# Late weight loads held back until tile 15 is transposed, engine orders judged under noise, and readout work moved from VectorE and ScalarE to GpSimd and VectorE

## The chip, the cores and the metric

The kernel runs on one core of one Trainium2 chip. Times are device microseconds (us). A time quoted for a kernel is the median of its runs; the span, which the profile shows, is about 1.7 us shorter and reaches from the first to the last instruction of one execution.

Engines in the profile lines: PE = TensorE matmuls, PEld = TensorE weight loads, DVE = VectorE, ACT = ScalarE, POOL = GpSimd, SP = the engine that issues most DMAs here.

## The reference

Two kinds of layer alternate, A, B, A, B, with the same weights in both rounds. `x` is [1, 2048, 512] in bf16; there are 32 heads of 16 elements; F is 1376.

```python
def _A_ref(x, wqkv, w_phi, wo):            # linear attention; H = 32, Dh = 16
    qkv = ...(x @ wqkv)...                 # q, k, v per head
    pq = einsum("bhsd,hdf->bhsf", q, w_phi); pk = einsum("bhsd,hdf->bhsf", k, w_phi)
    phi_q = concatenate([softmax(pq), softmax(-pq)], -1)
    phi_k = concatenate([softmax(pk), softmax(-pk)], -1)
    kv = einsum("bhsf,bhsd->bhfd", phi_k, v)
    z  = einsum("bhsf->bhf", phi_k)        # sum over all rows s
    num = einsum("bhqf,bhfd->bhqd", phi_q, kv)
    den = einsum("bhqf,bhf->bhq", phi_q, z)[..., None] + 1e-6
    return (num / den)...reshape(B, S, D) @ wo

def _B_ref(x, W_gate, W_up, W_down):
    gate = x @ W_gate; gate = gate * (gate > 0)
    return (gate * (x @ W_up)) @ W_down

x = A_x
x = x + _A_ref(_layernorm(x), ...);  x = x + _B_ref(_layernorm(x), ...)
x = x + _A_ref(_layernorm(x), ...);  x = x + _B_ref(_layernorm(x), ...)
```

The sum over all rows in `kv` divides each A layer in two. First comes a **key phase**, which ends with the last accumulation of `kv`; then a **readout**, which gives `num / den` tile by tile and feeds the **feed-forward** of layer B.

## The kernel before

The program works on 16 tiles of 128 rows. It is recorded as a list of operations, each with an engine, a modelled duration, and the things that it reads and writes. A list scheduler then makes one fixed order per engine: it tries 4 weights x 12 passes and keeps the order with the shortest modelled makespan.

```python
best = None
for weight in self.ORDER_WEIGHTS:
    prio = [weight * o.idx - rank[o.idx] - o.boost for o in ops]
    for _ in range(self.PASSES):
        start, finish, order = self._forward(prio)
        span = max(finish)                          # the judge
        if best is None or span < best[0]:
            best = (span, start, finish, order)
        prio = [t - o.boost for t, o in zip(self._backward(start, finish), ops)]
```

In the key phase of the first layer, VectorE makes layer-norm statistics and the softmax sums `Zk`, ScalarE the exponentials, and GpSimd multiplies by the reciprocal sums. The SP queue carries the DMA transposes of the normalised tiles (`yT`) and, between them, the weights that only later phases need.

```python
# knorm (per tile): sums and reciprocal on VectorE, then the product on GpSimd
op("dve", tensor_reduce(Zk, expk)); op("dve", reciprocal(rZk, Zk))
parts = [("pool", 0, 2)] if t < NT - 2 else [("pool", 0, 1), ("dve", 1, 2)]   # last two tiles split

def kv(t, n):                                       # emit(), layer 0
    ...
    for tt in range(t, t + n):
        self.kv_acc(tt, "A0")
        for _ in range(1 if 4 <= tt < 12 else 2):   # 8 wo, 4 Wg, 4 Wu, 6 Wd pieces
            if pieces:
                pieces.pop(0)(self.r("phik", tt, 0))
L(1); kv(0, 1); kv(1, 1); L(2); kv(2, 1); kv(3, 1); self.compose_q(); kv(4, 2)
L(3)                                                # layer norms and transposes, tiles 12 to 15
kv(6, 2); kv(8, 2); kv(10, 2); self.q_proj(0, qr0, "A0"); kv(12, 2); kv(14, 1); kv(15, 1)
```

The readout of one tile copies three groups of `num` out of PSUM on ScalarE, does the division on VectorE, transposes the result by DMA, and multiplies by `wo`.

```python
for gb in range(3):
    ...                                             # 8 matmuls in all
    op("act", activation(numbf[gb], psum, Copy))                         # numcp
op("dve", tensor_tensor(zm, nv, nr, mult))          # 64 columns
op("dve", tensor_tensor(zd, zm[0:32], zm[32:64], add))
op("dve", reciprocal(zr, zd))
op("dve", tensor_tensor(ab, nr, zr, mult))
op("dve", tensor_tensor(tsc, numbf, ab, mult))      # 1024 columns
op("dve", tensor_tensor(osb, tsc[0:512], tsc[512:1024], add))
self.dma_tr(oT <- osb)                              # SP queue
...                                                 # 4 matmuls with wo, residual add on VectorE
```

(The calls above are abridged; the names are the program's.)

The softmax here doesn't subtract the row's maximum and nothing guards it: scores larger than these inputs give would overflow.

## Time and profile before

| | before |
|---|---|
| time, median of 3 runs | 396.07 us (395.46 to 396.57) |
| span of the profiled execution | 394.1 us |
| last key accumulation, layer 0 (start of its last matmul; the modelled end is 0.22 us later) | 54.30 us |
| first gate matmul, layer 1 | 74.85 us |
| last key accumulation, layer 2 | 242.69 us |
| first gate matmul, layer 3 | 261.60 us |

The first line below is the busy time of each engine, from the page of the kernel before. The rows after it are the window view of the same execution: start and end of the stretch and its length, then busy us (and count of instructions) of PE, PEld, DVE, ACT and POOL, granted clock, share of the DMA engines, and GB/s.

```profile
PE 381.1 (97%) x2320; PEld 207.1 (53%) x2320; DVE 274.3 (70%) x634; ACT 215.8 (55%) x421; POOL 110.1 (28%) x160
...
15.00:55.00 40.00, 38.13 (x279) 20.89 (x277) 35.57 (x56) 31.92 (x48) 33.15 (x24) 1.00 0.66 161
55.00:65.00 10.00, 7.79 (x58) 4.13 (x57) 8.14 (x27) 8.79 (x17) 0.00 (x0) 1.00 0.18 43
65.00:76.00 11.00, 11.00 (x70) 5.98 (x68) 9.37 (x28) 10.43 (x16) 2.81 (x6) 1.00 0.30 60
76.00:240.00 164.00, 164.00 (x958) 88.13 (x957) 122.95 (x266) 75.54 (x159) 51.74 (x74) 1.00 0.18 34
240.00:257.00 17.00, 15.89 (x141) 9.71 (x139) 13.42 (x43) 13.73 (x25) 2.60 (x5) 1.00 0.16 32
257.00:270.00 13.00, 13.00 (x102) 9.07 (x100) 11.26 (x33) 11.52 (x25) 2.38 (x6) 1.00 0.34 65
```

TensorE has all of the 164 us in the middle. It has room in the key phase (15 to 55), in the first 10 us of the readout (55 to 65, where ScalarE is the busiest engine with 8.79 of 10 us), and in the same place of layer 2 (240 to 257).

Matmul ends are modelled, so a second measure is used throughout: the **loss**. That is the spacing of successive matmul starts beyond the normal spacing for their shape, summed over a window (the normal is the median in the trace of the kernel before: 216 ns for 128x512, 109 for 128x256, 63 for 128x144, 56 for 128x129 and 107 for the 128x128 ones, most of which come in the first 15 us). It is 12.8 us over the whole execution. The Trainium skill, "Perfetto Trace Analysis", Identifying the Most-Contended Engine, also calls matmul busy share a bad measure of how near a kernel is to its limit. This trace agrees in the small: 55 to 65 shows 2.2 us without a busy matmul, but 3.3 us of loss.

What TensorE waited for in the key phase, 15 to 55 us, from the view of waits (us in total, times, longest):

```profile
PE ps L587 <- DMA yT<-ytile: 1.2, 2, 0.9
PE ps L602 <- POOL expk L573: 0.3, 1, 0.3
```

And the starts of the readout in the timeline, 55 to 66 us (start, length, instruction, and in brackets the idle time before it with what ended it):

```profile
60.17 1.16 PE L645 MATMUL ps<-kvbd,expq 128*128 128x144 bf16 x8 [0.60 <-ACT numbf L649]
...
62.07 0.60 PE L675 MATMUL ps<-wo_p,oT 128*128 128x512 bf16 x2 [0.74 <-DMA oT<-osb]
...
64.22 0.60 PE L629 MATMUL ps<-yT,Wqp 128*128 128x512 bf16 x2 [0.68 <-ACT expq L632]
```

So the key phase waits for transposed tiles (L587 is the key projection), and at its end for GpSimd's product (L573). The readout waits twice for ScalarE (a `numbf` copy, an exponential `expq`) and once for a transposed output tile.

The costs that the argument needs, from the groups by shape (busy us and mean ns of one, then the idle time before):

```profile
L573 POOL TENSOR_TENSOR expk<-expk,rZk 128x1024 bf16<-128x1024 bf16 x28 | 53.6, 1933 | 30.1 <-DVE rZk L570 14.8 <-ACT expk L559 4.9 <-ACT vsb L561 4.3
...
L669 DVE TENSOR_TENSOR osb<-tsc 128x512 bf16<-128x512 bf16 x32 | 13.4, 418 | 0.2
L649 ACT ACTIVATE numbf<-ps 128x288 bf16<-128x288 f32 x32 | 13.4, 418 | 2.1 <-PE ps L645 2.1
```

### The profile page before, as it was taken

How to read it: one execution, taken by the hardware profiler on the slowest of the kernel's cores; microseconds unless marked ns; L12 is line 12 of the kernel's file. 1: busy time of each engine (PE TensorE's matmuls, PEld its weight loads, DVE VectorE, ACT ScalarE, POOL GpSimd, SP SyncE). 2: the span in 40 equal slices, each digit the busy share in tenths (PEclk: the TensorE clock that was granted, in tenths of full speed). 3: DMA queues.
4: the chain of work that ended last, by engine and by line, in shares of the span. 5: the costliest groups of instructions: out<-in, count | busy, mean ns of one | idle time of the engine just before them, and what ended most of it. 6: DMA issues, size and time to landing. Idle time of an engine off the chain costs nothing.

```text
span 394.1 us, 6313 instructions
## 1 busy us (share of the span) xinstructions
PE 381.1 (97%) x2320; PEld 207.1 (53%) x2320; DVE 274.3 (70%) x634; ACT 215.8 (55%) x421; POOL 110.1 (28%) x160
## 2 busy tenths in 40 slices
PE   5998997999999999999999999899999999999996
PEld 3455463676744444444444457467774454444442
DVE  5999778886865888886765777997875576421332
ACT  5897769953744412633354475997573562453440
POOL 5399741211000122383344543121101011100000
PEclk9999999999999999999999999999999999999999
DMA  6845942221211222311100110232323122100001
GB/s 189 217 86 147 240 146 53 55 54 28 55 28 27 42 54 54 68 27 15 27 14 2 27 28 2 41 68 54 68 55 67 27 42 67 29 27 0 28 27 53
DMA packets 61518, 23.00 MB, mean 58 GB/s; under 512 B 53456, under 2 KB 60464, under 8 KB 61488
## 3 DMA queue, kind: packets, MB, share of 16 engines
q1 hardware_dynamic: 60912, 22.08, 24.7%
q10 hardware_dynamic: 576, 0.52, 0.5%
q8 instruction: 18, 0.29, 0.3%
q14 instruction: 12, 0.10, 0.1%
HBM read 7.91 MB, written 2.10 MB: 25 GB/s over the span
## 4 chain that ended last, share of the span: by engine, by line
PE 83%; DVE 7%; issue 3%; DMA 3%; ACT 2%; POOL 2%; SPq 0%; DVEq 0%; POOLq 0%
PE ps L696 39%; PE ps L720 19%; PE ps L556 7%; PE ps L675 7%; PE ps L629 5%; PE ps L645 3%; PE ps L602 2%; DVE stats L516 2%; POOL expk L573 2%; DVE rZk L570 1%; DMA yT<-ytile 1%; DVE Zk L568 1%; DMA x_sb<-in_A_x_dram 1%; ACT numbf L649 1%; DMA oT<-osb 1%
## 5 line engine op out<-in xcount | busy, mean ns | idle before, releaser
L696 PE MATMUL ps<-yT,Wu 128*128 128x512 bf16 (+3 forms) x440 | 128.2, 336 | 0.0
L696 PE MATMUL ps<-yT,Wg 128*128 128x512 bf16 (+3 forms) x440 | 128.0, 336 | 0.0
L698 ACT ACTIVATE gate_sb<-ps 128x512 bf16<-128x512 f32 (+3 forms) x110 | 55.8, 512 | 100.8 <-PE ps L696 86.1
L720 PE MATMUL ps<-Wd,hT 128*128 128x512 bf16 (+1 forms) x352 | 107.7, 379 | 0.0
L573 POOL TENSOR_TENSOR expk<-expk,rZk 128x1024 bf16<-128x1024 bf16 (+1 forms) x32 | 59.6, 1879 | 31.6 <-DVE rZk L570 16.2
L520 POOL TENSOR_SCALAR rv<-mv 128x1 f32<-128x1 f32 (+1 forms) x55 | 13.0, 238 | 190.1 <-DVE mv L517 187.7
L696 PEld LDWEIGHTS ps<-yT,Wu 128*128 128x128 bf16 (+1 forms) x440 | 43.8, 100 | 33.4 <-ACT expk L703 0.8
L696 PEld LDWEIGHTS ps<-yT,Wg 128*128 128x128 bf16 (+1 forms) x440 | 43.5, 100 | 33.4 <-ACT gate_sb L698 0.9
L649 ACT ACTIVATE numbf<-ps 128x432 bf16<-128x432 f32 (+1 forms) x96 | 44.1, 500 | 18.1 <-PE ps L645 16.9
L720 PEld LDWEIGHTS ps<-Wd,hT 128*128 128x128 bf16 (+1 forms) x352 | 34.1, 98 | 36.8 <-DVE x_sb L722 0.9
L705 DVE TENSOR_TENSOR hT<-gate_sb,expk 128x512 bf16<-128x512 bf16 (+3 forms) x73 | 25.9, 355 | 34.2 <-ACT expk L703 33.0
L516 DVE BATCH_NORM_STATS2 stats<-x_sb 128x6 f32<-128x512 bf16 x64 | 42.7, 683 | 4.8 <-DMA x_sb<-in_A_x_dram 4.5
L568 DVE TENSOR_REDUCE Zk<-expk 128x64 f32<-128x1024 bf16 x32 | 37.9, 1202 | 6.3 <-ACT expk L559 3.1
L675 PE MATMUL ps<-wo_p,oT 128*128 128x512 bf16 x128 | 39.9, 379 | 1.6 <-DMA oT<-osb 1.6
L722 DVE TENSOR_TENSOR x_sb<-x_sb,ps 128x512 bf16<-128x512 bf16 x32 | 21.7, 685 | 27.1 <-PE ps L720 27.0
L703 ACT ACTIVATE expk<-ps 128x512 bf16<-128x512 f32 (+3 forms) x73 | 36.1, 497 | 1.1 <-PE ps L696 1.0
L645 PE MATMUL ps<-kvbd,expq 128*128 128x144 bf16 x256 | 35.1, 226 | 0.9 <-ACT numbf L649 0.6
L629 PE MATMUL ps<-yT,Wqp 128*128 128x512 bf16 x128 | 34.7, 379 | 0.9 <-ACT expq L632 0.7
L521 POOL TENSOR_TENSOR rstd<-rv,mhalf 128x1 f32<-128x1 f32 (+1 forms) x55 | 34.0, 620 | 4.1
L632 ACT ACTIVATE expq<-ps 128x1024 bf16<-128x1024 f32 (+1 forms) x40 | 32.4, 858 | 4.2 <-PE ps L629 3.8
L708 DVE TENSOR_TENSOR hT<-gate_sb,ps 128x512 bf16<-128x512 bf16 (+2 forms) x37 | 22.6, 614 | 16.8 <-PE ps L696 14.4
L559 ACT ACTIVATE expk<-ps 128x512 bf16<-128x512 f32 x44 | 23.8, 596 | 19.2 <-PE ps L556 18.9
(57 smaller groups left out, 393.3 us busy)
## 6 DMA issues: line engine op xcount, KB each, us to landing
out_dram<-x_sb SPq DMA_DIRECT2D x16, 128.0 KB, 1.7
x_sb<-in_A_x_dram SPq DMA_DIRECT2D x3, 512.0 KB, 6.1
Wg<-in_B_W_gate_dram SPq DMA_DIRECT2D x4, 344.0 KB, 4.2
Wu<-in_B_W_up_dram SPq DMA_DIRECT2D x4, 344.0 KB, 4.5
Wd<-in_B_W_down_dram SPq DMA_DIRECT2D x5, 256.0 KB, 3.3
yT<-ytile SPq DMA_TRANSPOSE x60, 2.4
hT<-in_A_wqkv_dram ACTq DMA_DIRECT2D x4, 128.0 KB, 3.0
x_sb<-in_A_x_dram SPq DMA_DIRECT2D x4, 128.0 KB, 3.7
```

Source lines behind the costliest of these rows:

```text
L516: op("dve", (lambda t: lambda e: e.bn_stats(k.stats6[:, t, :], k.x_sb[:, t, :]))(t), [r("x", t)], [r("st", t)], 685, f"{tag} stats {t}")
L521: op("pool", lambda e: e.tensor_tensor(k.rstd[:, t0:t1, :], k.rv1[:, t0:t1, :], k.mhalf[:, 0:n], ALU.pow), [r("rv1", t) for t in ts] + [r( ...
L568: op("dve", lambda e: e.tensor_reduce(k.Zk[:, zb, :], k.expk[:, t, :, :].rearrange("p s (h f) -> p (s h) f", f=16), AX.X, ALU.add), [r("ex ...
L573: op(eng, (lambda s0, s1: lambda e: e.tensor_tensor(k.expk[:, t, s0:s1, :].rearrange("p s (h f) -> p (s h) f", f=16), k.expk[:, t, s0:s1, ...
L629: op("pe", (lambda c, ic, bank: lambda e: e.matmul(k.pb[bank][:], k.Wqp[:, ic, c * 128:(c + 1) * 128], k.yT[:, ic, st * 512:(st + 1) * 512 ...
L645: op("pe", (lambda s, c, j, g0, bank: lambda e: e.matmul(k.pb[bank][:, j * GW:(j + 1) * GW], k.expq[:, st, c, s, tt * 128:(tt + 1) * 128], ...
L649: op("act", (lambda g0, n, bank: lambda e: e.activation(k.numbf[:, b, g0:g0 + n, :], k.pb[bank][:, 0:n * GW].rearrange("p (g m) -> p g m", ...
L675: op("pe", (lambda c, bank: lambda e: e.matmul(k.pb[bank][:], k.oT[:, ob, c, :], k.wo_p[:, c, :], start=(c == 0), stop=(c == NC - 1)))(c, ...
L696: op("pe", (lambda bank, W, ic, fc, Mf: lambda e: e.matmul(k.pb[bank][0:Mf, 0:n], W[:, ic, fc * 128:fc * 128 + Mf], k.yT[:, ic, c0:c0 + n] ...
L698: op("act", (lambda Mf, gb, gs: lambda e: e.activation(k.gate_sb[0:Mf, gs, 0:n], k.pb[gb][0:Mf, 0:n], ACT.Relu))(Mf, gb, gs), [self.RP[gb] ...
L703: op("act", (lambda Mf, ub, tu: lambda e: e.activation(k.expk[0:Mf, tu, 0, 0:n], k.pb[ub][0:Mf, 0:n], ACT.Copy))(Mf, ub, tu), [self.RP[ub] ...
L720: op("pe", (lambda fc, Kf, u, c0: lambda e: e.matmul(k.pb[bank][:], k.hT[0:Kf, u, c0:c0 + 128], k.Wd[0:Kf, fc, :], start=(fc == 0), stop=( ...
```

## The change

It has three parts. The *late weights* no longer depend on the tiles' products one by one: all of them wait for the transpose of tile 15. The *order* is judged by a replay under noise (six sets of durations, each within 8%) in place of the modelled makespan. In the *readout*, the third `numbf` copy goes from ScalarE to VectorE for every tile, and four small operations (`zm`, `zd`, `ab`, `osb`) go from VectorE to GpSimd from the third tile on.

```diff
@@ schedule
+        rng = random.Random(1)
+        noise = [[rng.uniform(0.92, 1.08) for _ in ops] for _ in range(self.TRIALS)]   # TRIALS = 6
-                span = max(finish)
+                span = self._replay(order, noise)
@@ num (calls cut)
-            op("act", activation(numbf, ..., Copy), 165 + n * 120, numcp)
+            op("dve" if gb == 2 else "act", evac(numbf, ...), 165 + n * (150 if gb == 2 else 120), numcp)
+        sm = "dve" if t < 2 else "pool"
-        op("dve", zm ...);  op("dve", zd ...);  op("dve", ab ...);  op("dve", osb ...)
+        op(sm, zm ...);     op(sm, zd ...);     op(sm, ab ...);     op(sm, osb ...)
@@ emit
             for tt in range(t, t + n):
                 self.kv_acc(tt, "A0")
-                for _ in range(1 if 4 <= tt < 12 else 2):
-                    if pieces:
-                        pieces.pop(0)(self.r("phik", tt, 0))
@@
         L(3)
+        for i, piece in enumerate(pieces):
+            piece(self.r("yT", 15 if i < 8 else 15))
```

(The body of `_replay` runs the fixed order through the model with scaled durations and returns the mean makespan.)

More of the change, by code (lines that the diff above doesn't have):

```diff
@@ L1 @@
+import random
 from contextlib import ExitStack
@@ L53 @@
     PASSES = 12
+    TRIALS = 6
     DMA_BW = 240.0
@@ L141, in schedule @@
                 prio = [t - o.boost for t, o in zip(self._backward(start, finish), ops)]
-        self.makespan, start, finish, order = best
+        _, start, finish, order = best
+        self.makespan = max(finish)
         for o in ops:
@@ L201, in _forward, with _replay @@
         return start, finish, order
+    def _replay(self, order, noise):
+        ops = self.ops
+        total = 0.0
+        for f in noise:
+            free = {e: 0.0 for e in ENG_NAMES}
+            fin = [0.0] * len(ops)
+            q_free = 0.0
+            for i in order:
+                o = ops[i]
+                t = free[o.eng]
+                for d in o.deps:
+                    t = max(t, fin[d] + (self.SAME_LAT if ops[d].eng == o.eng else self.SYNC_LAT))
+                free[o.eng] = t + o.dur * f[i]
+                if o.is_dma:
+                    q_free = max(t + self.DMA_FIXED * 0.35, q_free) + o.dma_bytes / self.DMA_BW * (3 * f[i] - 2)
+                    fin[i] = q_free + self.DMA_FIXED * 0.65 * (5 * f[i] - 4)
+                else:
+                    fin[i] = free[o.eng]
+            total += max(fin)
+        return total / len(noise)
     def _backward(self, start, finish):
@@ L335, with evac @@
 WINDOW = {"sp": 24, "act": 64, "pe": 400, "dve": 40, "pool": 24}
+def evac(e, out, in_):
+    return e.activation(out, in_, ACT.Copy) if hasattr(e, "activation") else e.tensor_copy(out, in_)
 class Kernel:
@@ L648, in num @@
                    [r("expq", st, c, s), r("kvbd", gb), r("kvones")], [self.RP[bank]], 63, f"{tag} num {t} {g0 + j}")
-            op("act", (lambda g0, n, bank: lambda e: e.activation(
-                k.numbf[:, b, g0:g0 + n, :], k.pb[bank][:, 0:n * GW].rearrange("p (g m) -> p g m", m=GW), ACT.Copy))(g0, n, bank),
-               [self.RP[bank]], [r("numbf", b, gb)], 165 + n * 120, f"{tag} numcp {t} {gb}")
+            op("dve" if gb == 2 else "act", (lambda g0, n, bank: lambda e: evac(
+                e, k.numbf[:, b, g0:g0 + n, :], k.pb[bank][:, 0:n * GW].rearrange("p (g m) -> p g m", m=GW)))(g0, n, bank),
+               [self.RP[bank]], [r("numbf", b, gb)], 165 + n * (150 if gb == 2 else 120), f"{tag} numcp {t} {gb}")
         RN = [r("numbf", b, gb) for gb in range(3)]
@@ L654, in num @@
         nr = nv[:, ::-1, :, 136:144]
-        op("dve", lambda e: e.tensor_tensor(
+        sm = "dve" if t < 2 else "pool"
+        op(sm, lambda e: e.tensor_tensor(
             k.zm[:, b, :].rearrange("p (s c h) -> p s c h", s=2, h=8), nv[:, :, :, 128:136], nr, ALU.mult),
-           RN, [r("zm", b, 0), r("zm", b, 1)], 222, f"{tag} zm {t}")
-        op("dve", lambda e: e.tensor_tensor(k.zd[:, b, :], k.zm[:, b, 0:32], k.zm[:, b, 32:64], ALU.add), [r("zm", b, 0), r("zm", b, 1)], [r("zd", b)], 190, f"{tag} zd {t}")
+           RN, [r("zm", b, 0), r("zm", b, 1)], 222 if sm == "dve" else 310, f"{tag} zm {t}")
+        op(sm, lambda e: e.tensor_tensor(k.zd[:, b, :], k.zm[:, b, 0:32], k.zm[:, b, 32:64], ALU.add), [r("zm", b, 0), r("zm", b, 1)], [r("zd", b)], 190 if sm == "dve" else 270, f"{tag} zd {t}")
         op("dve", lambda e: e.reciprocal(k.zr[:, b, :], k.zd[:, b, :]), [r("zd", b)], [r("zr", b)], 350, f"{tag} zr {t}")
-        op("dve", lambda e: e.tensor_tensor(
+        op(sm, lambda e: e.tensor_tensor(
             k.ab[:, b, :].rearrange("p (s c h) -> p s c h", s=2, h=8), nr,
             k.zr[:, b, :].rearrange("p (c h) -> p c h", h=8).unsqueeze(1).to_broadcast([P, 2, 4, 8]), ALU.mult),
-           RN + [r("zr", b)], [r("ab", b, 0), r("ab", b, 1)], 222, f"{tag} ab {t}")
+           RN + [r("zr", b)], [r("ab", b, 0), r("ab", b, 1)], 222 if sm == "dve" else 310, f"{tag} ab {t}")
         op("dve", lambda e: e.tensor_tensor(
@@ L668, in num @@
            RN + [r("ab", b, 0), r("ab", b, 1)], [r("tsc", b)], 690, f"{tag} tsc {t}")
-        op("dve", lambda e: e.tensor_tensor(k.osb[:, b, :], k.tsc[:, b, 0:512], k.tsc[:, b, 512:1024], ALU.add),
-           [r("tsc", b)], [r("osb", b)], 418, f"{tag} o {t}")
+        op(sm, lambda e: e.tensor_tensor(k.osb[:, b, :], k.tsc[:, b, 0:512], k.tsc[:, b, 512:1024], ALU.add),
+           [r("tsc", b)], [r("osb", b)], 418 if sm == "dve" else 1160, f"{tag} o {t}")
         ob = t % 4
```

## The prediction

> **What bounds the kernel now.** TensorE. The page shows it busy 97% of 394.1 us, but matmul ends are modelled, so I judge by the spacing of matmul starts in the trace (216 ns per 128x512 matmul): counting what exceeds normal spacing, TensorE loses 12.9 us, besides 3.1 us before its first matmul and 3.4 us after its last begins. (The Trainium skill, "Perfetto Trace Analysis", Identifying the Most-Contended Engine, also warns that matmul busy share says little.) Losses: 3.9 us in 0-15 us; 3.2 in 15-55 (key phase of layer 0: waits for transposed tiles at 30.8, 41.1, 44.8, for the last GpSimd normalisation at 53.9); 3.3 in 55-65 (start of the readout: waits of 0.60 for numbf, 0.74 for oT, 0.68 for expq in the timeline); 1.9 in 245-257 (the same in layer 2); 0.5 in all the rest. From 65 to 240 us TensorE has no gap. So no order can win more than 3%; the realistic prize lies in 15-65 us.
>
> **What the change does.** No matmul is added or removed.
> (a) Late weights. Before, wo/Wg/Wu pieces (0.33-0.67 us of issue each, timeline) stand between the yT transposes (1.2-1.3 us each) on the SP queue from 21.7 to 40 us. After, ten transposes stand ahead of all weights, three wo pieces between the last two. 4.7 MB at some 235 GB/s (seen in 40-55 us) is an estimated 20 us, done near 57-60. wo is needed near 62, Wg near 75: nothing should starve.
> (b) Order. Until the key accumulation ends TensorE's work is the same; it can end no earlier than 54.5 - 3.2 = 51.3 us. VectorE now does all layer-norm statistics before the second Zk, so GpSimd's 16 normalisations (1.93 us each) start near 21.5 instead of 19.0 but then run unbroken: 21.5 + 0.5 + 14 x 1.93 + 2 x 0.98 = 51 us; VectorE comes out near 50.5. I expect the end at 52-53 instead of 54.5: 1.5-2 us won.
> (c) Readout. VectorE loses zm, zd, ab, osb (220+182+221+418 ns) for 14 of 16 tiles per layer and gains the third numbf copy from ScalarE (418 ns there). GpSimd gains an estimated 2.0-2.5 us per tile (osb: half of 1933 ns, or the 1500 ns that its 128x512 shape showed beside VectorE), 55-65 us in all, on an engine 28% busy. ScalarE, 88% busy in 55-65, sheds 0.4 us per tile: about 0.5-1 us off the readout ramps. Elsewhere the relief is worth nothing, TensorE having no gaps. Cost: oT comes 1-2 us later per tile, and VectorE can block. The Trainium skill, "SBUF — State Buffer", Who interferes with whom, says a VectorE instruction with two SBUF inputs contends with a GpSimd one that reads SBUF, and the loser waits it out; the 1500 ns agrees. I allow 0.3 us of new gaps.
>
> Sum: -1.8 (a, b) - 0.9 (c) + 0.3, about -2.5 us: **393.4 us**, 80% range 390.7 to 396.3. Faster by over 2%: 0.03; within 2%: 0.95; slower by over 2%: 0.02.
>
> **What would show it.** Key accumulation ending at 52-53 us; no TensorE wait for yT at 30-45 us; GpSimd unbroken from 22 to 51; TensorE gapless through both feed-forward stages; GpSimd busy 165-175 us, VectorE about 260, ScalarE about 203; osb on GpSimd 1.0-1.5 us.
>
> **What would make it wrong.** Slower: weights in flight when the first oT transposes are issued (TensorE waiting over 1 us on oT, or on wo), tile 6's transpose late because its apply stands behind more statistics, or GpSimd readouts blocking the gate product so that gaps appear after 65 us. Faster: both ramps closing completely, down to about 389.

## The result and the profile after

The changed kernel took 394.37 us (4 runs, 394.27 to 394.40), and the kernel before 395.94 us beside it (4 runs). The ratio is 0.9959, with a 95% interval from 0.9942 to 0.9976. A ratio here is the mean time of one kernel's fast runs over that of the other's of the same rounds, so not quite the ratio of the medians quoted. A second set of runs on another chip (below, "the changed kernel again") gave 0.9949. The gain is real and small: about 0.4 to 0.5%, or 1.6 to 2 us.

The trace of the first profiled execution lacks 43 matmul records, so sums of TensorE time are read from the second one, which has all 2320. The same milestones in both:

| us | before | changed | changed, again |
|---|---|---|---|
| start of the last key accumulation, layer 0 | 54.30 | 53.59 | 54.22 |
| from there to the first gate matmul | 20.55 | 19.40 | 19.39 |
| from there to the last key accumulation, layer 2 | 167.84 | 167.83 | 167.84 |
| from there to the first gate matmul, layer 3 | 18.91 | 18.29 | 18.28 |
| from there to the end | 132.55 | 133.56 | 133.50 |

Each row counts from the one above it, so the columns add up to spans of 394.15, 392.67 and 393.23 us. (The repeat's profiled run was its slowest, 394.96 us by the clock; the median of its six runs is 393.94.) The 168 us in the middle did not move by a hundredth. Both readouts are shorter, by 1.2 and 0.6 us, the key phase is shorter by 0.1 to 0.7, and the last part is 1.0 us *longer*. (Two later runs, e9 and e10, have the same TensorE order and the same key phase; their accumulations came at 53.69 and 53.68 us. So 54.22 is the odd one of four, and about 0.5 of it had been lost by 15 us already.)

The same windows as before, for the changed kernel's second profile (columns as above):

```profile
PE 380.1 (97%) x2320; PEld 206.8 (53%) x2320; DVE 267.5 (68%) x554; ACT 207.1 (53%) x389; POOL 166.7 (42%) x272
...
15.00:55.00 40.00, 38.27 (x281) 21.36 (x279) 37.18 (x58) 32.02 (x48) 33.56 (x26) 1.00 0.57 156
55.00:65.00 10.00, 8.98 (x68) 5.04 (x67) 7.88 (x25) 8.26 (x14) 2.16 (x6) 1.00 0.31 83
65.00:76.00 11.00, 10.55 (x73) 6.25 (x71) 9.18 (x22) 10.26 (x17) 7.09 (x15) 1.00 0.30 61
76.00:240.00 164.00, 163.98 (x963) 87.86 (x962) 120.59 (x233) 72.15 (x144) 74.71 (x117) 1.00 0.17 34
240.00:257.00 17.00, 16.80 (x131) 9.78 (x129) 13.60 (x36) 13.95 (x22) 6.37 (x14) 1.00 0.16 32
257.00:270.00 13.00, 11.87 (x99) 8.83 (x98) 9.96 (x26) 9.08 (x22) 8.36 (x17) 1.00 0.45 73
```

TensorE won 1.2 us in 55 to 65 and 0.9 in 240 to 257. It lost 0.45 in 65 to 76 and 1.1 in 257 to 270, where it had had no gap. The losses by spacing of starts, each put in the window in which the spacing begins, for the changed kernel and those experiments whose traces are complete (e7 and e11 left out):

| loss, us, in window | before | changed, again | four tiles on VectorE (e6) | copy alone, no noise (e8) | frozen order, layer-2 pair (e9) | frozen order, all on VectorE (e10) | old weights (e12) |
|---|---|---|---|---|---|---|---|
| 0-15 | 4.0 | 4.5 | 3.3 | 4.7 | 4.3 | 3.7 | 4.3 |
| 15-55 | 3.2 | 3.0 | 4.3 | 2.2 | 2.7 | 3.2 | 3.7 |
| 55-65 | 3.3 | 1.2 | 1.9 | 1.7 | 1.2 | 1.2 | 1.4 |
| 65-76 | 0.0 | 0.6 | 1.7 | 1.5 | 0.6 | 1.0 | 0.6 |
| 76-240 | 0.2 | 0.5 | 0.2 | 1.2 | 0.5 | 0.8 | 0.2 |
| 240-257 | 1.9 | 0.6 | 0.6 | 0.6 | 0.7 | 0.7 | 0.6 |
| 257-270 | 0.0 | 1.5 | 1.0 | 0.5 | 1.4 | 1.6 | 0.7 |
| 270-end | 0.2 | 0.2 | 0.6 | 0.2 | 0.2 | 0.2 | 0.2 |

The changed kernel, e9 and e10 do the same on TensorE, in the same order; where they differ before 55 us (3.7 to 4.5, and 2.7 to 3.2) is what one execution differs from the next.

**Key phase.** TensorE's waits in 15 to 55 us in the first profile after (the projection is now L618, its exponential L621, the accumulation L633):

```profile
PE ps L618 <- ACT expk L621: 1.2, 2, 1.0
PE ps L618 <- DMA yT<-ytile: 0.3, 1, 0.3
PE ps L633 <- POOL expk L604: 0.2, 1, 0.2
```

The transposes' 1.2 us became 0.3, as intended (0.7 in the repeat), but another wait of 1.2 us, for ScalarE, stands in their place (0.8 in the repeat). The median landing of the last two `yT` transposes of the phase shows the intent at work: first before (36 to 46 us), then after (35 to 42 us); the last number is us from issue to landing.

```profile
yT<-ytile SPq DMA_TRANSPOSE x2, 4.9
```

```profile
yT<-ytile SPq DMA_TRANSPOSE x2, 2.6
```

What the phase ends on is GpSimd's chain of products. What GpSimd waited for from 18 to 54 us, before and then after:

```profile
POOL expk L573 <- ACT expk L559: 1.6, 1, 1.6
...
POOL expk L573 <- DVE rZk L570: 0.6, 1, 0.6
```

```profile
POOL expk L604 <- DVE rZk L601: 1.5, 4, 0.7
```

The chain before runs from 18.99 to 53.82 us with 2.66 us idle; after, from 21.42 to 53.24 us with 1.52 us idle. It starts 2.4 us later and ends only 0.6 us earlier. In the repeat, TensorE's last accumulation came just 0.1 us earlier than before.

**Readout.** In the timeline of the first profile after, 55 to 76 us, TensorE's idle stretches are these:

```profile
59.66 0.82 PE L660 MATMUL ps<-yT,Wqp 128*128 128x512 bf16 x3 [0.68 <-ACT expq L663]
...
63.60 1.04 PE L660 MATMUL ps<-yT,Wqp 128*128 128x512 bf16 x4 [0.17 <-ACT expq L663]
...
72.99 0.27 PE L728 MATMUL ps<-yT,Wg 128*128 128x256 bf16 x1 [0.44 <-DMA yT<-ytile]
```

The waits for `numbf` and `oT` are gone. By what ended them, the losses over 0.1 us of the first readout (55 to 66 us) and of layer 2's (240 to 257 us) are these; e1 and e2, described below, have the copy on ScalarE as before but another order, and are rough, their traces being incomplete:

| loss, us | before | e1 | e2 | changed, again | e6 and e8 |
|---|---|---|---|---|---|
| layer 0: `numbf` / `expq` | 1.2 / 0.9 | 1.2 / 0.7 | 1.0 / 0.6 | 0 / 1.2 | 1.0 / 0.5 |
| layer 0: `oT` | 0.9 | 0 | 0.2 at most | 0 | 0 |
| layer 2: `numbf` / `expq` | 0.5 / 0.3 | 0.5 / 0.3 | 0.5 / 0.7 | 0 / 0.5 | 0 / 0.5 |
| layer 2: `oT` | 1.0 | 1.0 | 0 | 0 | 0 |

So the waits for ScalarE fell from 2.1 to 1.2 us and from 0.8 to 0.5, 1.2 us together, and the rest of what the readouts won is two waits for `oT`, of 0.9 and 1.0 us. The first of them is all but gone in e1 and e2 too, where the readout is untouched: another order is enough to take it away. (By the windows above the first readout won 0.2 us more, and the key phase 0.3 less: a wait for VectorE of 0.2 to 0.3 us before the first `num` matmul begins at 55.0 us before and at 54.9 after, on the other side of the window's edge.)

There is a new wait at the very first gate matmul (L728), for a transposed tile that lands at 72.85 us. Before, TensorE came to that matmul at 74.85 and found it ready.

**Layer 2.** The largest new gap lies near 263 us. The weight loads of the first profile after show it (the matmul of L707 is among the missing records):

```profile
262.70 0.10 PEld L728 LDWEIGHTS ps<-yT,Wu 128*128 128x128 bf16 x1
263.94 0.10 PEld L707 LDWEIGHTS ps<-wo_p,oT 128*128 128x128 bf16 x1 [1.15 <-DMA oT<-osb]
```

TensorE stands for about 1.2 us before the `wo` product of the fifth tile. Its `oT` transpose was issued at 259.63 us and landed 4.27 us later (4.21 in the repeat), where transposes usually take 2.43. The DMA view of the first profile after, 258 to 265 us (queue and kind: packets, MB, share; then issues and their median us to landing):

```profile
q8 instruction: 1, 0.02, 1.4%
...
oT<-osb SPq DMA_TRANSPOSE x2, 3.8
```

A packet of the instruction queue (16,384 bytes) began at 260.77 us, 1.1 us after that transpose's issue, and took 1.57 us. At the usual 2.43 us the tile would have landed at 262.06, before TensorE came to it.

**VectorE beside GpSimd.** The groups by shape after, for the lines shown above (`osb` is L701, the third copy L366), and the gate product (L737), whose mean before was 423 ns:

```profile
L701 POOL TENSOR_TENSOR osb<-tsc 128x512 bf16<-128x512 bf16 x28 | 32.7, 1168 | 21.3 <-DVE tsc L696 18.2 <-DVE mv L548 3.1
...
L737 DVE TENSOR_TENSOR hT<-gate_sb,expk 128x512 bf16<-128x512 bf16 x35 | 15.5, 444 | 26.0 <-ACT expk L735 25.9
...
L366 DVE CAST numbf<-ps 128x288 bf16<-128x288 f32 x32 | 14.6, 455 | 12.2 <-PE ps L676 12.0
```

`osb` takes 1168 ns on GpSimd against 418 on VectorE. A few gate products take nearly three times as long as usual, and each of these began during an `osb` of GpSimd; the timeline at 299 us shows one:

```profile
299.34 1.15 POOL L701 TENSOR_TENSOR osb<-tsc 128x512 bf16<-128x512 bf16 x1 [0.92 <-DVE tsc L696]
...
299.59 1.18 DVE L737 TENSOR_TENSOR hT<-gate_sb,expk 128x512 bf16<-128x512 bf16 x1 [0.40 <-ACT expk L735]
```

This is what the Trainium skill, "SBUF — State Buffer", Who interferes with whom, says of a VectorE instruction with two SBUF inputs beside a GpSimd one that reads SBUF: the second to come waits it out. Here the pair came to 1.18 us, against about 0.42 alone.

### The profile page after: what moved, and what is told of

It reads as the page before. It is cut to its first block, busy times and chain, and to the rows that moved or that the text cites. A ratio compares the mean times of both kernels' runs of the same rounds, so it can differ in the third digit from the quotient of the medians.

```text
span 392.7 us, 6311 instructions
## 1 busy us (share of the span) xinstructions
PE 377.3 (96%) x2277; PEld 206.9 (53%) x2320; DVE 267.4 (68%) x554; ACT 207.1 (53%) x389; POOL 166.4 (42%) x272
## 4 chain that ended last, share of the span: by engine, by line
PE 84%; DVE 5%; POOL 4%; DMA 2%; ACT 2%; issue 2%; SPq 0%; DVEq 0%; ACTq 0%; POOLq 0%
PE ps L728 39%; PE ps L752 19%; PE ps L587 7%; PE ps L707 6%; PE ps L660 5%; PE ps L676 4%; POOL expk L604 3%; DVE stats L547 2%; PE ps L633 2%; PE ps L618 2%; DMA yT<-ytile 1%; DMA x_sb<-in_A_x_dram 1%; POOL rstd L552 1%; DVE ytile L564 1%; ACT expq L663 1%
## 5 line engine op out<-in xcount | busy, mean ns | idle before, releaser
L728 PE MATMUL ps<-yT,Wg 128*128 128x512 bf16 (+3 forms) x435 | 125.9, 336 | 2.0 <-ACT numbf L366 1.1
L728 PE MATMUL ps<-yT,Wu 128*128 128x512 bf16 (+3 forms) x436 | 124.2, 336 | 0.4
L752 PE MATMUL ps<-Wd,hT 128*128 128x512 bf16 (+1 forms) x340 | 104.0, 379 | 0.6
L728 PEld LDWEIGHTS ps<-yT,Wg 128*128 128x128 bf16 (+1 forms) x440 | 43.7, 100 | 34.4 <-issue 1.5
L728 PEld LDWEIGHTS ps<-yT,Wu 128*128 128x128 bf16 (+1 forms) x440 | 43.7, 100 | 33.4 <-ACT expk L735 0.8
L737 DVE TENSOR_TENSOR hT<-gate_sb,expk 128x512 bf16<-128x512 bf16 (+3 forms) x73 | 28.7, 393 | 31.0 <-ACT expk L735 30.2
L366 ACT ACTIVATE numbf<-ps 128x432 bf16<-128x432 f32 x64 | 32.9, 538 | 17.7 <-PE ps L676 17.4
L701 POOL TENSOR_TENSOR osb<-tsc 128x512 bf16<-128x512 bf16 x28 | 32.7, 1168 | 21.3 <-DVE tsc L696 18.2
L707 PE MATMUL ps<-wo_p,oT 128*128 128x512 bf16 x122 | 38.7, 379 | 0.2
L660 PE MATMUL ps<-yT,Wqp 128*128 128x512 bf16 x121 | 33.6, 379 | 1.2 <-ACT expq L663 1.0
L552 POOL TENSOR_TENSOR rstd<-rv,mhalf 128x1 f32<-128x1 f32 (+1 forms) x55 | 33.1, 607 | 3.1
```

What stands on the lines that cost most here:

```text
L552: op("pool", lambda e: e.tensor_tensor(k.rstd[:, t0:t1, :], k.rv1[:, t0:t1, :], k.mhalf[:, 0:n], ALU.pow), [r("rv1", t) for t in ts] + [r( ...
L660: op("pe", (lambda c, ic, bank: lambda e: e.matmul(k.pb[bank][:], k.Wqp[:, ic, c * 128:(c + 1) * 128], k.yT[:, ic, st * 512:(st + 1) * 512 ...
L707: op("pe", (lambda c, bank: lambda e: e.matmul(k.pb[bank][:], k.oT[:, ob, c, :], k.wo_p[:, c, :], start=(c == 0), stop=(c == NC - 1)))(c, ...
L728: op("pe", (lambda bank, W, ic, fc, Mf: lambda e: e.matmul(k.pb[bank][0:Mf, 0:n], W[:, ic, fc * 128:fc * 128 + Mf], k.yT[:, ic, c0:c0 + n] ...
L752: op("pe", (lambda fc, Kf, u, c0: lambda e: e.matmul(k.pb[bank][:], k.hT[0:Kf, u, c0:c0 + 128], k.Wd[0:Kf, fc, :], start=(fc == 0), stop=( ...
```

## The experiments

The theory at the start was that ScalarE's relief shortens the readouts, that the late weights shorten the key phase, and that the new gaps come from the longer latency of GpSimd's small operations. The rivals were that the new order (or its noisy judge) does the work, and that the weights do nothing.

### e1: the late weights alone

```diff
 (kernel before, with only this of the change)
-                for _ in range(1 if 4 <= tt < 12 else 2): ...
+        for i, piece in enumerate(pieces):
+            piece(self.r("yT", 15 if i < 8 else 15))
```

> The kernel before with the late-weights part alone. My theory (each part has a cause of its own): the key accumulation of layer 0 ends about 0.7 us sooner than before, as in the changed kernel, the readout ramps lose as much as before, so the time is 395.3 us against 395.9. Rival 1 (the noisy judge found the better order): nothing without it, 395.9. Rival 2 (every rebuild of the order scatters by about 1 us, whatever the part): anywhere in 395 to 397.

Measured: 395.33 us against 396.43, ratio 0.997 (0.995 to 0.9989). The last key accumulation came at 54.66 us, not earlier than the 54.30 of before, so the time was forecast rightly, but the gain isn't where the theory put it. By loss (this trace lacks some 42 matmul records, so the figure is rough) the gain lies in the first readout, about 2.2 us in place of 3.3, which the weights don't touch directly. The order of all engines had been made anew. What follows: a part that is tried alone brings its own order with it.

### e2: the noise judge alone

```diff
-                span = max(finish)
+                span = self._replay(order, noise)
```

> The kernel before with the noisy judge alone. My theory: no cost is removed, so 395.9 within 0.5. Rival 1: most of the gain of 1.5 us is here, 394.5. Rival 2: anywhere in 395 to 397.

Measured: 396.29 us, ratio 0.9996 (0.9978 to 1.0014). The judge by itself is worth nothing that can be seen. Yet its order loses only 2.0 to 2.2 us in 55 to 65 (rough, as in e1) in place of 3.3, with the copy still on ScalarE.

### e3: the readout alone

```diff
+            op("dve" if gb == 2 else "act", evac(numbf, ...))
+        sm = "dve" if t < 2 else "pool"      # zm, zd, ab, osb
```

> The kernel before with the readout part alone (numbf copy to VectorE, smalls to GpSimd). My theory: the ramp of layer 0 loses about 1.5 us less than before because ScalarE is relieved, and layer 2 gives some back because oT of the first GpSimd tiles comes late: 395.0 us. Rival 1: 395.9. Rival 2: anywhere in 394 to 397.

Measured: 395.60 us, ratio 0.9998 (0.9965 to 1.0031). Two of the six runs (397.71 and 398.83) ran at a granted clock of 0.995; the other four lie between 394.59 and 395.85. The first readout's loss was about 1.1 us (a rough sum, as in e1), as in the changed kernel. So the ramp closes with the readout part alone (and the order that came with it), but the ratio is too blurred to put a price on it.

### e4: the changed kernel without the noise judge

```diff
-                span = self._replay(order, noise)
+                span = max(finish)
```

> The changed kernel with the order judged as before, without noise. My theory: 394.4 us as the changed kernel, within 0.5. Rival 1: the gain goes, 395.5 or more. Rival 2: anywhere in 393.5 to 396.5.

Measured: 393.65 us, ratio 0.9936 (0.9917 to 0.9955). It is at least as good as the changed kernel. Its last key accumulation came at 52.62 us, inside the 52 to 53 that the prediction had expected of the changed order, though by another way: its GpSimd chain started at 18.7 and not 21.5 us, and ran to 51.70 with 0.79 us idle. Its only difference from e3 is the position of the late weights: 55.63 us there, 52.62 here, and the intervals of the two ratios don't overlap. It loses time again in layer 2, by the same kind of late `oT`:

```profile
263.73 0.49 PE L728 MATMUL ps<-yT,Wg 128*128 128x256 bf16 x3 [1.67 <-DMA oT<-osb]
```

That `oT` took 4.30 us; TensorE lost 1.83 us by it.

### e5: the changed kernel again

No edit; it runs beside e6, e7 and e8.

> The changed kernel, unedited, as the measure for the other three of this set on the same chip. Expected: 0.996 of before, as first measured; if the noisy judge cost 0.6 us by itself, it is slower than its copy without the judge, of which the last set gave 0.9936.

Measured: 393.94 us against 396.23, ratio 0.9949 (0.9927 to 0.997). The profile was complete; its lines are shown above. The gaps near 73 and 263 us were there again at the same places, so they belong to the order and not to a single execution.

### e6: four tiles kept on VectorE

The theory of the moment was that the new gaps at the first gate matmuls come from GpSimd's latency in tiles 2 and 3.

```diff
-        sm = "dve" if t < 2 else "pool"
+        sm = "dve" if t < 4 else "pool"
```

> The changed kernel with the smalls of the first four tiles, not two, left on VectorE. My theory: TensorE's 1.25 us wait at 262.8 us is for the oT of the fourth tile, late by its chain on GpSimd, so this wait and most of the 0.6 us at 72.2 us go, and the time falls by 1.2 to 1.8 us against the changed kernel: 0.992 of before. Rival: VectorE is what is short in the ramps, and four tiles on it open the waits there again: 0.996 or more.

Measured: 396.67 us, ratio 1.0011 (0.999 to 1.0032), slower than the changed kernel. The theory fell, or at least the test did: the edit remade the order, and this order waits 1.77 us for a transposed tile in the key phase, which the readout cannot have caused. The waits of 36 to 44 us:

```profile
PE ps L618 <- DMA yT<-ytile: 1.6, 1, 1.6
```

That transpose was issued at 37.63 us and took 3.76 us, with an instruction packet in flight; at 2.43 us the loss would have been an estimated 0.45.

### e7: the same without the noise judge

```diff
-                span = self._replay(order, noise)
+                span = max(finish)
-        sm = "dve" if t < 2 else "pool"
+        sm = "dve" if t < 4 else "pool"
```

> The same with the order judged as before, without noise. My theory: the wait of 1.8 us for oT that the copy without noise showed near 262 us goes as well: 392 us, 0.990 of before, the fastest yet. Rival (order alone scatters by 1 us): no better than 0.9936.

Measured: 397.28 us, ratio 1.0038 (1.0012 to 1.0064), where 0.990 was expected; two of six runs were at a clock of 0.996, and the profiled one is one of them. In it the granted clock was 0.5 for 3.4 us from 95.1 us on, an estimated 1.7 us of TensorE's time; the wait that follows lies before that and isn't part of it. Even its fastest run, 396.42 us, is slower than all of e5. Here is a single wait of 2.14 us at 92.8 us, in the middle of the feed-forward, where no other kernel has one. The waits of 90 to 98 us, and two lines of the DMA view of 90 to 96 us:

```profile
PE ps L707 <- DMA oT<-osb: 2.0, 1, 2.0
```

```profile
q8 instruction: 1, 0.02, 1.2%
...
oT<-osb SPq DMA_TRANSPOSE x1, 4.2
```

Again one 16,384-byte instruction packet, and a transpose that takes 4.23 us. That turned the attention from GpSimd to the transposes.

### e8: only the copy moved, no noise judge

```diff
-                span = self._replay(order, noise)
+                span = max(finish)
-        sm = "dve" if t < 2 else "pool"
+        sm = "dve"
```

> Late weights and the third numbf copy on VectorE, but every small stays on VectorE; judged without noise. My theory: what closes the readout ramp is ScalarE's relief, so the ramp of layer 0 loses as little as in the changed kernel (about 1.2 us in 55 to 65) and no oT wait appears near 262: as fast as with the smalls of the first four tiles on VectorE, 0.990. Rival (VectorE's relief closes the ramp): the ramp loses 2.5 us or more and the time is 0.995 or more.

Measured: 396.53 us, ratio 1.002 (0.9992 to 1.0049); two runs at a clock of 0.996, the other four from 395.49 to 396.90. The ramp at 55 to 65 closed to 1.7 us with nothing of the readout on GpSimd, near the 1.2 of the theory. But 1.0 us of waits for `numbf` stayed there, though the copy was moved, and TensorE lost about as much as was won at the first gate matmul (waits of 54 to 78 us):

```profile
PE ps L728 <- DMA yT<-ytile: 1.3, 1, 1.3
PE ps L676 <- ACT numbf L366: 0.3, 1, 0.3
```

So the total gave nothing, where the theory had 0.990. This gap occurs with none of the small operations on GpSimd, so their latency isn't needed to make it.

### e9: the changed kernel's order frozen, two tiles of layer 2 back on VectorE

From here on the order was made with the change's assignment, and only afterwards was an operation given to another engine. It keeps its place in the global list from which each engine's order is taken, so the order of everything else stays what it was.

```diff
             prog.schedule()
+            for x in prog.ops:
+                w = x.name.split()
+                if x.eng == "pool" and len(w) == 3 and w[1] in ("zm", "zd", "ab", "o") \
+                        and w[0] == "A2" and w[2] in ("2", "3"):
+                    x.eng = "dve"
```

> The changed kernel with its order frozen as scheduled; afterwards only zm, zd, ab and osb of the third and fourth tile of layer 2 are handed to VectorE, at the same place in the order. TensorE's order is the same, so nothing is reshuffled. My theory: TensorE's wait near 263 us (1.0 to 1.25 us, for the oT of the fourth tile) goes and nothing comes in its place: about 1.1 us under the changed kernel, 0.992 of before. Rival (VectorE is what is short there): the wait only changes its name, 0.995.

Measured: 393.82 us against 396.52, ratio 0.9936 (0.9919 to 0.9954). The two waits in question, from the timeline of 259 to 265 us:

```profile
259.63 0.27 PE L728 MATMUL ps<-yT,Wg 128*128 128x256 bf16 x1 [0.66 <-issue]
...
263.95 0.39 PE L707 MATMUL ps<-wo_p,oT 128*128 128x512 bf16 x1 [0.36 <-DMA oT<-osb]
```

By loss, the wait near 264 fell to 0.52 us and the one at 258.6 grew from 0.48 to 0.82; the window 257 to 270 went from 1.5 to 1.4. So the wait was moved, hardly removed. And my reading was wrong: the awaited `oT` is the fifth tile's, which this edit leaves on GpSimd, not the fourth's. It took 3.94 us to land.

### e10: the same frozen order, all small operations on VectorE

```diff
-                        and w[0] == "A2" and w[2] in ("2", "3"):
+                        and True:
```

> The same frozen order with all smalls of both layers back on VectorE; the third numbf copy stays on VectorE. If relief of VectorE closes the readout ramp of layer 0, the loss of 1.8 us in 55 to 76 grows to 3 us or more, and the time is 0.997 or more. If ScalarE's relief closes it, as I predicted, that loss stays below 2 us, the wait near 263 us goes, and the time is 0.992.

Measured: 395.42 us, ratio 0.9978 (0.9961 to 0.9994). It ran in the same rounds as e9, has the same order (TensorE's and ScalarE's instructions follow each other just as in e5 and e9), and the intervals don't overlap. So in this order the small operations on GpSimd are worth about 0.4%. (A reservation: the order was made with GpSimd's durations in mind.) The two profiled executions differ by less than the medians, 0.86 us of span, and the milestones place all of it: 0.4 up to the first gate matmul, 0.3 in the middle, 0.2 at the end. By its own expectation e10 falls between the branches: 55 to 76 lost 2.2 us (below 2 was one, 3 or more the other), the wait near 263 us stayed, and the ratio is the rival's. Three readings come from it.

First, the loss at 55 to 65 stays at 1.2 us: in this order VectorE's relief isn't needed to close the ramp. (That ScalarE's relief closes it is not shown by this: the copy stays on VectorE here as in e9, and no run gave it back to ScalarE in the frozen order.) Second, the waits in layer 2 stay, with nothing of the readout on GpSimd:

```profile
260.30 0.27 PE L728 MATMUL ps<-yT,Wg 128*128 128x256 bf16 x1 [0.56 <-issue]
...
264.82 0.39 PE L707 MATMUL ps<-wo_p,oT 128*128 128x512 bf16 x1 [0.56 <-DMA oT<-osb]
```

So GpSimd's small operations aren't needed to make them; that `oT` took 4.40 us. Third, the gate product is back at 421 ns from 445 (128x512) and at 276 from 326 (128x256): with the order held, only GpSimd's work was taken away, so this slowing is shown to be GpSimd's, 2.9 us of VectorE's time over the kernel (28.8 us of gate products in e5, 25.9 here).

### e11: frozen pair in the order without noise

```diff
-                span = self._replay(order, noise)
+                span = max(finish)
+            (the loop of e9)
```

> The copy of the changed kernel judged without noise (0.9936 of before), its order frozen, with the smalls of the third and fourth tile of layer 2 handed to VectorE. My theory: its wait of 1.8 us for oT near 262 us goes: about 392.3 us, 0.990 of before, better than both kernels. Rival: 0.9936 or more.

Measured: 393.87 us, ratio 0.9937 (0.9918 to 0.9956), no better than e4's 0.9936. The wait near 263 was still 1.30 us, and a new one of 0.62 came at 251.5.

### e12: the changed kernel with the old weight positions

```diff
+                for _ in range(1 if 4 <= tt < 12 else 2):
+                    if pieces:
+                        pieces.pop(0)(self.r("phik", tt, 0))
-        for i, piece in enumerate(pieces):
-            piece(self.r("yT", 15 if i < 8 else 15))
```

> The changed kernel with the late weights put back behind the normalisations, as before. My theory: the key accumulation of layer 0 ends where it did before (54.5 us and not 53.8) and the time is 0.6 to 1.2 us over the changed kernel: 0.9975 of before. Rival (order scatters by 1 us whatever the part): anywhere from 0.993 to 1.000, with the loss or gain in stages that the weights do not touch.

Measured: 394.83 us, ratio 0.9969 (0.995 to 0.9988). The last key accumulation came at 55.3 us (53.6 to 54.2 with late weights), and the loss in 15 to 55 was 3.7 us (3.0 in e5, 2.7 in e9). The last two `yT` transposes took 4.04 and 5.18 us amid weights, where they take 2.6 with late ones. The direction is the one predicted. The size, 1 us or so, is within what another order may do, since this kernel's order was rebuilt too, and its interval overlaps that of e9.

Seven of the eight combinations of the three parts were run, so each part has three pairs that differ in it alone (ratios, without it and with it):

| part | pairs |
|---|---|
| late weights | 1 to 0.997 (e1); 0.9998 (e3) to 0.9936 (e4); 0.9969 (e12) to 0.9949 (e5) |
| readout | 1 to 0.9998 (e3); 0.997 (e1) to 0.9936 (e4); 0.9996 (e2) to 0.9969 (e12) |
| noise judge | 1 to 0.9996 (e2); 0.9998 (e3) to 0.9969 (e12); 0.9936 (e4) to 0.9949 (e5) |

Every pair brings an order of its own, and most of the steps are no larger than their intervals. Still, the late weights gain in all three, which is the best sign that they are worth something.

### What these orders have in common: late transposes

The kernels with a rebuilt order lie between 393.65 and 397.28 us, with single waits for a transposed tile in different places. In all 14 profiled executions together, I sorted the `yT` and `oT` transposes issued after 60 us by whether an instruction packet (8 to 16 KB) was in flight between 1.0 and 2.4 us after their issue:

| | transposes | took over 3 us |
|---|---|---|
| no instruction packet in that time | 913 | 1 |
| one in flight | 197 | 121 |

The usual time is 2.43 us, and a late one takes 3 to 5. Packets of 16 KB take 0.9 to 1.7 us. They are those of the queue q8, the larger of the two instruction queues; there are 18 in an execution, and in the same order they come at nearly the same places. With one of them in flight 95 of 116 transposes were late, with packets of 8 KB alone 26 of 81. The Trainium skill, "DMA: Bandwidth & Descriptors", Queues, rings and completion order, says that a DMA engine takes turns between queues a whole packet at a time, which would explain why a transpose, whose shares lie on many engines, ends with the one that was held up. The table shows that the two go together. No run here moved an instruction packet on purpose, so the cause is argued, not shown; and the account is not complete, for in 83 of the 121 late cases the delay beyond 2.43 us is over 0.1 us longer than the packet (1.8 us beside a packet of 1.2 in e7). What is measured are the waits: 1.2 us in the changed kernel, 1.83 in e4, 2.14 in e7 and 1.77 in e6, where the usual landing time would have left an estimated 0, 0, 0.3 and 0.45.

No version clearly beats the changed kernel. e4, e9 and e11, at 0.9936 to 0.9937, overlap with its 0.9949 and 0.9959.

## Why the prediction was right, and where its steps were wrong

The time came out at 394.37 us against a predicted 393.4, inside the range and in the class that had 95%. The bound was read rightly: with 12.8 us of loss no order could bring much. But that class and that range (390.7 to 396.3) would have held no effect at all, 395.94 us, as well, and the sum came out near the mark by luck: errors with different signs nearly cancel.

| term, us | predicted | measured (loss, before to changed again) |
|---|---|---|
| key phase (a, b) | -1.8 | -0.1 (3.2 to 3.0; -0.5 without the wait at the window's edge, but 0.5 more was lost before 15 us); by the start of the last accumulation -0.1, and -0.6 to -0.7 in three other executions |
| readout ramps (c) | -0.9 | -2.1 (3.3 to 1.2) and -1.3 (1.9 to 0.6) |
| new gaps | +0.3 | +0.6 (65-76) and +1.5 (257-270) |
| in all | -2.5 | -0.8 over all windows, those outside these rows included; -0.9 (again) and -1.5 by the two spans; -1.6 by the medians |

**The key phase failed.** The step was that GpSimd's normalisations "then run unbroken", to end at 51 us, and the accumulation with them at 52 to 53 (54.5 before; the modelled ends are 53.8 and, again, 54.4). They were broken four times, 1.5 us in all, by VectorE's reciprocals; and the two half-size ones at the end took about 1.4 us each, though the sum put in 0.98 while its next paragraph quoted 1500 ns for just that shape. The chain ended at 53.24 us. That the waits for transposes would shrink was right (1.2 to 0.3 us, 0.7 in the repeat), but a wait for ScalarE of 1.2 us (0.8) took their place. That no weights would be missed was right: the ramp after shows no wait for `wo` or `Wg`.

**The ramps' mechanism agrees with the trace; what they won beyond it was not foreseen.** The readouts won 3.4 us of loss by the windows and 3.1 by what ended the waits, not 0.9. But the waits that ended on ScalarE fell by 1.2 us in both layers together, near the 0.9 of the prediction; the other part, 1.9 us, is the two waits for `oT`, whose end the prediction did not count in (it had listed the first among the losses), and the first goes with a new order alone (e1, e2). Complete traces with the third copy on VectorE lose 1.2 to 1.9 us in 55 to 65, against 3.3 before and a rough 2.0 to 2.2 in the two new orders that keep the copy on ScalarE. How much of the difference is ScalarE's relief and how much the order's stays open, since no run put the copy back in a frozen order.

**The allowance for new gaps was mis-sized**, 0.3 for 2.1 us. The sentence "TensorE gapless through both feed-forward stages" failed near 73, at 258.6 and near 263 us. The reason that the prediction named for such gaps (later `oT` by GpSimd, VectorE blocked) is not the one that the runs support: with every small operation on VectorE the gaps near 73, 259 and 264 us stayed in the same order (e10), and the first of them in another (e8). TensorE came earlier to the same transposes, and one of them is late together with an instruction packet.

**"Elsewhere the relief is worth nothing" is not borne out** in this order: e10 against e9 gives about 0.4% for the small operations on GpSimd. Of the 0.86 us by which the two profiled executions differ, about 0.5 arises after the first gate matmul, outside the first ramp.

**Indicators.** GpSimd busy 166.4 us (165 to 175 expected), `osb` 1.17 us (1.0 to 1.5), ScalarE 207 (203): right or near. VectorE 267 in place of 260: about 5 of the 7 us are gate products (28.6 us in all, 25.9 before) and layer-norm applications (27.7, 25.5 before) that got slower. VectorE did block, as was named; no wait of TensorE was traced to it. The noise judge, to which the prediction gave no term, has none (0.9996 alone, and 0.9936 with it taken out).

**Open:** how much of the readouts' gain is the moved copy's and how much the new order's; whether an instruction packet delays a transpose or merely comes with it; the wait of about 0.5 us at 258.6 us, which the profile puts down to nothing; and how much of the late weights' gain is theirs and how much their order's (the key phase got no shorter by them in e1, some 1 us in e12 and 3.0 us from e3 to e4).

## What to carry to other kernels

Where a scheduler fixes the order, a part of a change cannot be priced by rebuilding the kernel without it, since rebuilt orders here differed by 2.7 us with nearly the same parts (e5 and e6: two tiles of small operations); make the order first, and then move the operation to the other engine. Look for the engine that is busiest in the stretch where TensorE waits (ScalarE at the start of the readout), not the one that is busiest on average, and expect that when its wait goes, the next latency in the stretch shows, here a DMA transpose. When one transpose is late at the same place in every run, look whether an instruction packet is in flight beside it before blaming the engine that fed it.

## What the Trainium skill lacked or had wrong

- "DMA: Bandwidth & Descriptors", DMA Transpose (X-bar), gives no landing time. Here a 128x512 bf16 transpose from SBUF to SBUF lands 2.43 us after issue, and in 3 to 5 us in 121 of 197 cases with an instruction packet in flight (1 of 913 without).
- "Runtime: NRT & Kernel Launch", Instruction fetch mechanics, calls the cost of the 16 KiB refills "mostly hidden". Packets of 16,384 bytes on an instruction queue are seen here, each of 0.9 to 1.7 us; where one coincided with a transpose that TensorE needed, TensorE stood for up to 2.1 us. That the refill is the cause was not tried.
- "GPSIMD Engine Reference", Performance versus the Vector engine, gives 1.96x for a `tensor_tensor` add in fp32. The bf16 add of 128x512 took 1168 ns on GpSimd and 418 on VectorE, 2.8x.
- "SBUF — State Buffer", Who interferes with whom, is confirmed (1.18 us for a gate product beside an `osb`, against about 0.42; with GpSimd's work taken away under the same order, the mean of the 128x512 ones fell from 445 to 421 ns). It doesn't give the size over a kernel: 2.9 us of VectorE's gate products here.
